# Holding back one transposing load until a weight slice has landed, in a two-layer SiLU block with gradients

## The chip, the cores and the metric

The kernel runs on one core of one Trainium2 chip. The metric is the device time of one execution in microseconds (us), the median over several executions. The profiler's span of an execution is shorter than its time (318.8 against 320.54 for the kernel before); in what follows "span" and "at 18.4 us" are the profile's clock.

## The reference

x is (2048, 640), w1 (640, 1536), w2 (1536, 640), all bf16. The outputs are the result of the block and the gradients for x, w1 and w2.

```python
def _fwd_reference(x, w1, w2):
    h = jnp.einsum("bsd,df->bsf", x, w1)
    h = _silu(h)
    out = jnp.einsum("bsf,fd->bsd", h, w2)
    return out
# reference(): out and the vjp of grad_out for x, w1, w2
```

## The kernel before

The rows of x are worked off in four chunks of 512. For the first chunk the kernel does not wait for one big transposed load: it loads 256 rows plainly and transposes them on TensorE (first half), and gets the other 256 rows (second half) by a transposing DMA. w1 comes in five row slices (k = 0 to 4, the first in two pieces), so that the matmuls of slice k can start as soon as it is there. All loads but two come from the SyncE queue, in the order of the program text:

```python
early += [load_x(nc.sync, 0), load_x(nc.scalar, 1)]
early += [load_w1(0, slice(0, F // 2)), load_w1(0, slice(F // 2, F), nc.scalar)]
early += [load_w1(k) for k in range(1, 3)]
for k in range(3, DT):
    load_w1(k)
nc.sync.dma_start_transpose(out=xT_next[:, :, HC:SC], in_=x2[HC:SC, :])   # second x half
# ...
nc.sync.dma_start(out=w2_nat[:], in_=w2_v[:])                             # w2, 1920 KB
goT_next = load_goT(0)                                                    # transposing
for fc in range(NFC):
    nc.sync.dma_start_transpose(out=w2T[:, :, fc * FC:(fc + 1) * FC], in_=w2[...])
nc.sync.dma_start_transpose(out=w1T[:], in_=w1[:, :])
```

TensorE works through them so (cut):

```python
def h_first(xT, aT, ghT):
    pe_x(xT)                                   # 10 transposes of the first half
    for dt_ in range(DT):                      # first half: slice by slice of w1
        for pair in range(NPAIR):
            h_pair_mm(hs[0][pair], pair, dt_, xT, halves[0])      # 12 matmuls per slice
    # ...
    for pair in range(NPAIR):                  # second half: 60 matmuls, need all of w1 and xT
        for q in range(2):
            for dt_ in range(DT):
                h_pair_mm(hp, pair, dt_, xT, halves[1], (q,))
# then
sd_phase(c, w2_nat, aT, oT_scr)                # "oT" matmuls: the first ones that need w2
```

Of the kernel before, what the change touches and what calls it, by code (L numbers as in the profile page):

```python
# [15 lines left out]
def start_before_entry_wait(nc, names):  # L16




    def move(nc):
        blocks = nc.m.functions[0].blocks
        entry, home = blocks[0].instructions, blocks[1].instructions
        for engine in {i.engine for i in home if i.name in names}:
            mine = [i for i in home if i.engine == engine]
            last = max(k for k, i in enumerate(mine) if i.name in names)
            moved = mine[: last + 1]
            gate = next(
                k
                for k, i in enumerate(entry)  # L30
                if i.engine == engine and isinstance(i, mybir.InstEventSemaphore)
            )
            taken = {i.name for i in moved}
            for k in reversed(range(len(home))):
                if home[k].name in taken:
                    del home[k]
            for i in reversed(moved):
                entry.insert(gate, i)

    nc.at_finalize(move)  # L40


def last_stores_end_on_pool(nc, names):




    def move(nc):
        blocks = nc.m.functions[0].blocks
        stores = [next(i for b in blocks for i in b.instructions if i.name == name) for name in names]  # L50
        lanes = [u.id for i in stores for u in i.sync_info.on_update]
        end = blocks[-1].instructions
        at = next(k for k, i in enumerate(end) if i.engine == mybir.EngineType.SP)
        waits = list(end[at].sync_info.on_wait)
        late = [w for lane in reversed(lanes) for w in waits if w.id == lane]
        assert len(late) == len(names) and not end[at].sync_info.on_update
        waits = [w for w in waits if w.id not in lanes]
        end[at] = copy.replace(end[at], sync_info=mybir.SyncInfo(on_wait=waits, on_update=[]))
        pool = [i for i in end if i.engine == mybir.EngineType.Pool]
        drain, gather, release, reset, clear, drain2, gather2, release2 = pool  # L60
        assert gather2.sync_info.on_wait and not release2.sync_info.on_wait
        assert all(i.sync_info is None or not i.sync_info.on_wait for i in (reset, clear, drain2))
        closing = {i.name for i in (reset, clear, drain2, gather2)}
        to = next(k for k, i in enumerate(end) if i.name == reset.name)
        for k in reversed(range(len(end))):
            if end[k].name in closing:
                del end[k]
        reset = copy.replace(reset, sync_info=mybir.SyncInfo(on_wait=late, on_update=[]))
        for i in (drain2, clear, reset, gather2):
            end.insert(to, i)  # L70

    nc.at_finalize(move)

# [2 lines left out]
def kernel(  # L76
# [11 lines left out]
    nc = tc.nc  # L88
    P = 128
    x2 = x.flatten_outer_dims()  # L90
# [7 lines left out]
    ST, DT, FT = S // P, D // P, F // P  # L98
    SC = 512
# [7 lines left out]
    HC = 2 * P  # L107
# [38 lines left out]
    with ExitStack() as mctx:  # L146
# [9 lines left out]
        early = [nc.vector.memset(warm[:], 1.0)]  # L156
# [13 lines left out]
        def load_xT(c):  # L170
            xT = xpool.tile([P, DT, SC], dt_in, name="xT")
            nc.sync.dma_start_transpose(out=xT[:], in_=x2[c * SC:(c + 1) * SC, :])
            return xT
# [6 lines left out]
        xT_next = xpool.tile([P, DT, SC], dt_in, name="xT")  # L180
# [4 lines left out]
        def load_w1(k, cols=slice(0, F), eng=nc.sync):  # L185
            return eng.dma_start(out=w1_nat[:, k, cols], in_=w1_v[:, k, cols])  # L186
# [1 line left out]
        early += [load_x(nc.sync, 0), load_x(nc.scalar, 1)]  # L188
        early += [load_w1(0, slice(0, F // 2)), load_w1(0, slice(F // 2, F), nc.scalar)]
        early += [load_w1(k) for k in range(1, 3)]  # L190
        for k in range(3, DT):
            load_w1(k)
        nc.sync.dma_start_transpose(out=xT_next[:, :, HC:SC], in_=x2[HC:SC, :])
        start_before_entry_wait(nc, {i.ins.name for i in early})
        nc.scalar.activation(warm_a[:], warm[:, 0:1], ACT.Silu)
        nc.sync.dma_start(out=w2_nat[:], in_=w2_v[:])
# [133 lines left out]
        for c in range(NCH):  # L330
# [4 lines left out]
            if c + 1 < NCH:  # L335
                xT_next = load_xT(c + 1)
# [9 lines left out]
            if c == 0:  # L346
                h_first(xT, aT, ghT)
                nc.sync.dma_start(
                    out=aT_scr[:, c * SC:(c + 1) * SC].rearrange("(ft p) s -> p ft s", p=P), in_=aT[:]
                )  # L350
                sd_phase(c, w2_nat, aT, oT_scr)
                for ft in range(FT):
                    g_group(ft, goT, ghT)
                nc.sync.dma_start(
                    out=ghT_scr[:, c * SC:(c + 1) * SC].rearrange("(ft p) s -> p ft s", p=P), in_=ghT[:]
# [4 lines left out]
            for i in range(FT + LAG):  # L360
# [7 lines left out]
                out=aT_scr[:, c * SC:(c + 1) * SC].rearrange("(ft p) s -> p ft s", p=P), in_=aT[:]  # L368
            )
            nc.sync.dma_start(  # L370
                out=ghT_scr[:, c * SC:(c + 1) * SC].rearrange("(ft p) s -> p ft s", p=P), in_=ghT[:]
# [7 lines left out]
    with ExitStack() as fctx:  # L379
# [17 lines left out]
        k = 0  # L397
# [26 lines left out]
        k = 0  # L424
        for fc in range(NFC):
            gh_blk = gh_blks[fc]
            for dt_ in range(DT):
                if dt_ == DT // 2:
                    store_gw2(fc)
                if fc == NFC - 1 and dt_ == DT - 1:  # L430
                    last_stores = []
                    for k, (lo, hi) in enumerate(((0, FC - P), (FC - P, FC))):
                        gp = ps_h.tile([P, FC], FP32, name="hp")
                        for st in range(ST):
                            nc.tensor.matmul(  # L435
                                gp[:, lo:hi],
                                lhsT=x_nat[:, st, dt_ * P:(dt_ + 1) * P],
                                rhs=gh_blk[:, st, lo:hi],
                                start=(st == 0),
                                stop=(st == ST - 1),  # L440
                            )
                        g1 = s1pool.tile([P, FC], dt_in, name="g1")
                        if k == 0:
                            nc.scalar.activation(g1[:, lo:hi], gp[:, lo:hi], ACT.Copy)
                        else:
                            nc.vector.tensor_copy(out=g1[:, lo:hi], in_=gp[:, lo:hi])  # L446
                        store = nc.sync.dma_start(
                            out=gw1_v[:, dt_, fc * FC + lo:fc * FC + hi], in_=g1[:, lo:hi]
                        )
                        last_stores.append(store.ins.name)  # L450
                    last_stores_end_on_pool(nc, last_stores)
                    continue
# [46 lines left out]
```

## Time and profile before

| | kernel before |
|---|---|
| time, median of 3 runs | 321.04 us (320.81 to 322.33) |
| span of the profiled run | 318.8 us |
| TensorE busy | 313.6 us |
| slice k=2 landed / TensorE waits for it | 7.88 / 0.65 us |
| second x half landed / wanted | 11.12 / 11.76 us |
| w2 landed / first oT matmul | 17.91 / 18.41 us |

The table's landing times come from the trace's records of the semaphore increments (a load counts as landed with the last of its 16), the rest from the views. The prediction below shows the page's lines, the chain of waits and the SyncE queue. One more view is TensorE's timeline of the kernel before, with start, length, line, operation, what, and in brackets the idle time ahead of it and who ended it. L246 are the h matmuls, L315 the oT matmuls.

```profile
5.79 1.48 PE L246 MATMUL hp<-xT,w_nat 128*128 128x256 bf16 x12 [0.22 <-DMA w_nat<-in_w_dram]
7.92 10.65 PE L246 MATMUL hp<-xT,w_nat 128*128 128x256 bf16 x96 [0.65 <-DMA w_nat<-in_w_dram]
18.41 3.83 PE L315 MATMUL hp<-aT,w_nat 128*128 128x512 bf16 x16
```

w2 and w1 carry the same name here (w_nat).

### The profile page before, as it was taken

The numbers are of one execution on the slowest core, as the hardware profiler recorded it, in microseconds if no ns is written. First come the engines' busy times: TensorE is split into PE (matmuls) and PEld (weight loads), VectorE is DVE, ScalarE is ACT, GpSimd is POOL, SyncE is SP. The second block draws the span as 40 slices with busy tenths as digits, with TensorE's granted clock in tenths as the row PEclk, the third lists the DMA queues.
The fourth block names the chain that finished last, engine by engine and source line by source line (L and its number), as shares of the span: only waits on it lengthen the run. The fifth ranks groups of instructions, "written<-read, shape, count | busy, mean of one in ns | idle before, by whom it ended". The sixth has DMA issues, their size and how long they took to land.

```text
span 318.8 us, 3632 instructions
## 1 busy us (share of the span) xinstructions
PE 313.6 (98%) x1516; PEld 150.5 (47%) x1544; DVE 102.8 (32%) x182; ACT 76.8 (24%) x139; POOL 0.7 (0%) x6
## 2 busy tenths in 40 slices
PE   8999999999999999999999999999999999999997
PEld 6854444444444444444444444444444444444444
DVE  1495641477410087710147741000000100001001
ACT  2691000545201354411054520110100001001010
POOL 0000000000000000000000000000000000000000
DMA  8999999999989986492635079909999999997111
GB/s 280 293 181 192 221 249 260 349 252 280 292 214 343 230 155 176 169 310 76 168 110 141 0 256 267 221 20 297 211 245 254 204 251 326 236 313 217 65 35 49
DMA packets 147233, 67.02 MB, mean 210 GB/s; under 512 B 113937, under 2 KB 146705, under 8 KB 147217
## 3 DMA queue, kind: packets, MB, share of 16 engines
q1 hardware_dynamic: 146928, 66.43, 83.3%
q10 hardware_dynamic: 288, 0.36, 0.3%
q8 instruction: 12, 0.20, 0.2%
q14 instruction: 5, 0.03, 0.0%
HBM read 9.18 MB, written 28.97 MB: 120 GB/s over the span
## 4 chain that ended last, share of the span: by engine, by line
PE 96%; DMA 2%; issue 1%; SPq 0%; DVE 0%; DVEq 0%
PE hp L315 32%; PE hp L299 16%; PE hp L404 16%; PE hp L455 15%; PE hp L217 12%; PE hp L246 3%; DMA w_nat<-in_w_dram 2%; PE hp L435 1%; SPq L186 0%; SPq L183 0%; DVE g L446 0%; DVEq L446 0%; SPq L483 0%
## 5 line engine op out<-in xcount | busy, mean ns | idle before, releaser
L299 PE MATMUL hp<-goT,w2T 128*128 128x512 bf16 x239 | 56.8, 379 | 0.1
L315 PE MATMUL hp<-ghT,w1T 128*128 128x512 bf16 x235 | 52.2, 379 | 0.3
L315 PE MATMUL hp<-aT,w_nat 128*128 128x512 bf16 x234 | 52.1, 379 | 0.3
L404 PE MATMUL hp<-a_blk,go_nat 128*128 128x512 bf16 x235 | 51.7, 379 | 0.3
L455 PE MATMUL hp<-gh_blk,x_nat 128*128 128x512 bf16 x219 | 48.2, 379 | 0.3
L217 PE MATMUL hp<-xT,w_nat 128*128 128x512 bf16 x174 | 43.4, 379 | 0.3
L323 ACT ACTIVATE oT<-hp 128x512 bf16<-128x512 f32 x24 | 14.5, 604 | 106.8 <-PE hp L315 106.8
L299 PEld LDWEIGHTS <-w2T 128*128 128x128 bf16 x240 | 23.5, 98 | 28.3
L404 PEld LDWEIGHTS <-go_nat 128*128 128x128 bf16 x240 | 23.5, 98 | 28.3
L315 PEld LDWEIGHTS <-w1T 128*128 128x128 bf16 x240 | 23.4, 98 | 28.4
L315 PEld LDWEIGHTS <-w_nat 128*128 128x128 bf16 x240 | 23.5, 98 | 28.1
L306 DVE SCALAR_TENSOR_TENSOR ghT<-ghT,hp 128x512 bf16<-128x512 bf16 x48 | 32.5, 683 | 7.3 <-PE hp L299 7.3
L455 PEld LDWEIGHTS <-x_nat 128*128 128x128 bf16 x224 | 21.9, 98 | 26.4
L325 DVE CAST oT<-hp 128x512 bf16<-128x512 f32 x16 | 11.1, 691 | 72.2 <-PE hp L315 67.7
L226 ACT ACTIVATE aT<-hp 128x512 bf16<-128x512 f32 x36 | 21.5, 597 | 30.4 <-PE hp L217 30.4
L217 PEld LDWEIGHTS <-w_nat 128*128 128x128 bf16 x180 | 17.6, 98 | 21.2
L233 DVE SCALAR_TENSOR_TENSOR ghT<-aT,v 128x512 bf16<-128x512 bf16 x36 | 24.7, 686 | 0.2
L232 DVE TENSOR_SCALAR v<-t 128x512 bf16<-128x512 f32 x36 | 15.4, 427 | 26.7 <-ACT t L230 26.7
L230 ACT ACTIVATE t<-hp 128x512 f32<-128x512 f32 x36 | 21.3, 591 | 0.0
L466 DVE CAST g<-hp 128x512 bf16<-128x512 f32 x7 | 4.8, 692 | 47.0 <-PE hp L455 27.0
L414 DVE CAST g2T<-hp 128x512 bf16<-128x512 f32 x7 | 4.8, 692 | 46.1 <-PE hp L404 46.1
L412 ACT ACTIVATE g2T<-hp 128x512 bf16<-128x512 f32 x8 | 4.8, 597 | 47.0 <-PE hp L404 47.0
(28 smaller groups left out, 76.4 us busy)
## 6 DMA issues: line engine op xcount, KB each, us to landing
aT_scr<-aT SPq DMA_DIRECT2D x4, 1536.0 KB, 6.3
ghT_scr<-ghT SPq DMA_DIRECT2D x4, 1536.0 KB, 8.2
out_dram<-o_sb SPq DMA_DIRECT2D x8, 640.0 KB, 3.3
oT_scr<-oT SPq DMA_DIRECT2D x4, 640.0 KB, 3.6
go_nat<-in_grad_out_dram SPq DMA_DIRECT2D x4, 640.0 KB, 8.1
gxT_scr<-oT SPq DMA_DIRECT2D x4, 640.0 KB, 4.8
w_nat<-in_w_dram SPq DMA_DIRECT2D x1, 1920.0 KB, 11.0
x_nat<-in_x_dram SPq DMA_DIRECT2D x3, 640.0 KB, 7.4
```

Source lines behind the costliest of these rows:

```text
L217: nc.tensor.matmul(hp[:], lhsT=w1_nat[:, dt_, ft * P:(ft + 1) * P], rhs=xT[:, dt_, :], start=(dt_ == 0), stop=(dt_ == DT - 1),)
L226: nc.scalar.activation(aT[:, ft, :], hp[:], ACT.Silu)
L230: nc.scalar.activation(t[:], hp[:], ACT.Tanh, scale=0.5)
L232: nc.vector.tensor_scalar(out=v[:], in0=t[:], scalar1=-0.5, scalar2=0.5, op0=ALU.mult, op1=ALU.add)
L233: nc.vector.scalar_tensor_tensor(out=ghT[:, ft, :], in0=aT[:, ft, :], scalar=1.0, in1=v[:], op0=ALU.subtract, op1=ALU.mult)
L299: nc.tensor.matmul(gp[:], lhsT=w2T[:, dt_, ft * P:(ft + 1) * P], rhs=goT[:, dt_, :], start=(dt_ == 0), stop=(dt_ == DT - 1),)
L306: nc.vector.scalar_tensor_tensor(out=ghT[:, ft, :], in0=ghT[:, ft, :], scalar=1.0, in1=gp[:], op0=ALU.add, op1=ALU.mult)
L315: nc.tensor.matmul(op_[:], lhsT=w_all[:, ft, dt_ * P:(dt_ + 1) * P], rhs=rhs_all[:, ft, :], start=(ft == 0), stop=(ft == FT - 1),)
L323: nc.scalar.activation(oT[:, dt_, :], op_[:], ACT.Copy)
L325: nc.vector.tensor_copy(out=oT[:, dt_, :], in_=op_[:])
L404: nc.tensor.matmul(gp[:], lhsT=go_nat[:, st, dt_ * P:(dt_ + 1) * P], rhs=a_blk[:, st, :], start=(st == 0), stop=(st == ST - 1),)
L455: nc.tensor.matmul(gp[:], lhsT=x_nat[:, st, dt_ * P:(dt_ + 1) * P], rhs=gh_blk[:, st, :], start=(st == 0), stop=(st == ST - 1),)
```

## The change

The intent: the second x half isn't wanted before 11.8 us, the w1 slices are wanted at once. If the descriptors of the early-issued transposing load (its orders for the single pieces) stand in the way of the w1 slices, hold that load back until the third slice (k=2) has landed. With the change, the lines stand 25 lower (L246 is L271, L315 is L340, L196 is L221), the transposing load itself 24 (L193 is L217).

```diff
+def issue_after_landing(nc, name, load_name):
+    def move(nc):
+        insts = [i for b in nc.m.functions[0].blocks for i in b.instructions]
+        load = next(i for i in insts if i.name == load_name)
+        (lane,) = {u.id for u in load.sync_info.on_update}
+        first = min(
+            (w for i in insts if i.sync_info is not None for w in i.sync_info.on_wait if w.id == lane),
+            key=lambda w: w.wait_value,
+        )
+        # ... adds `first` to the waits of the instruction `name`
+    nc.at_finalize(move)
...
-        for k in range(3, DT):
-            load_w1(k)
-        nc.sync.dma_start_transpose(out=xT_next[:, :, HC:SC], in_=x2[HC:SC, :])
+        late = [load_w1(k) for k in range(3, DT)]
+        x_late = nc.sync.dma_start_transpose(out=xT_next[:, :, HC:SC], in_=x2[HC:SC, :])
+        issue_after_landing(nc, x_late.ins.name, early[-1].ins.name)
```

More of the change, by code (lines that the diff above doesn't have):

```diff
@@ L70, in move @@
             end.insert(to, i)
+    nc.at_finalize(move)
[8 more added lines that the diff above has]
+        )
+        for block in nc.m.functions[0].blocks:
+            for k, i in enumerate(block.instructions):
+                if i.name == name:
+                    have = i.sync_info
+                    waits = [] if have is None else list(have.on_wait)
+                    updates = [] if have is None else list(have.on_update)
+                    assert all(w.id != lane for w in waits)
+                    block.instructions[k] = copy.replace(
+                        i, sync_info=mybir.SyncInfo(on_wait=waits + [first], on_update=updates)
+                    )
     nc.at_finalize(move)
```

## The prediction

> **What bounds the kernel now.** I read the page first, then the chain of waits in order of time, then the waits by engine, then the first 32 us of the timeline by engine, and last the landing times of the single DMAs.
>
> The page says where a change can count at all:
>
> ```profile
> span 318.8 us, 3632 instructions
> PE 313.6 (98%) x1516; PEld 150.5 (47%) x1544; DVE 102.8 (32%) x182; ACT 76.8 (24%) x139; POOL 0.7 (0%) x6
> PE 96%; DMA 2%; issue 1%; SPq 0%; DVE 0%; DVEq 0%
> ```
>
> TensorE is busy 313.6 of 318.8 us, so only 5.2 us are idle in the whole kernel, start and tail included. No change to a load can win more than that, and one that wins 2% (6.4 us) is out of reach. The 2% of DMA on the chain that ended last is the part to look at. In order of time the chain reads:
>
> ```profile
> 1.47 6.41 DMA w_nat<-in_w_dram
> 7.88 0.05 issue
> 7.92 10.65 PE hp L246 x96
> ...
> 18.84 10.74 PE hp L315 x49
> ...
> 31.53 8.85 PE hp L299 x41
> ```
>
> The columns are start, length, what. The DMA is the third w1 row slice (k=2), issued at 1.47 and landed at 7.88. From 7.92 on TensorE runs through with gaps of hundredths of a us. So anything that moves 7.92, or opens a gap after it, reaches the end one for one. The waits of the first 40 us give the size of what there is to win:
>
> ```profile
> PE hp L246 <- DMA w_nat<-in_w_dram: 0.9, 2, 0.7
> ```
>
> TensorE waits 0.22 us for slice k=1 (before 5.79) and 0.65 us for slice k=2 (before 7.92), together 0.87 us. The queue of SyncE is the other half of the story; in its timeline the columns are start, length of the issue, what:
>
> ```profile
> 0.54 2.31 SPq L186 DMA_DIRECT2D w_nat<-in_w_dram  x5
> 3.09 3.79 SPq L193 DMA_TRANSPOSE xT<-in_x_dram  x1
> 6.94 0.58 SPq L196 DMA_DIRECT2D w_nat<-in_w_dram  x1
> 7.56 10.61 SPq L177 DMA_TRANSPOSE goT<-in_grad_out_dram  x1
> 18.21 10.18 SPq L199 DMA_TRANSPOSE w2T<-in_w_dram  x3
> 28.43 9.14 SPq L200 DMA_TRANSPOSE w1T<-in_w_dram  x1
> ```
>
> The transposing load of the second x half is issued at 3.09, right behind slices k=3 and k=4, its issue occupies the queue for 3.79 us, and it lands 8.0 us after its start, at 11.1. All of it is in-order: the w2 load starts only at 6.94.
>
> **What the Trainium skill says.** "Perfetto Trace Analysis", section "DMA Instruction — HWDGE (DVE, Sync)", says that the profiled length of such an issue is descriptor generation, that the data movement [...]is not in it. The trace agrees: L193 is 3.79 us long and lands 4.2 us after its end. "DMA: Bandwidth & Descriptors", section "Queues, rings and completion order", says that one copy is split over the rings of up to 16 engines and that each ring consumes its descriptors in order. The trace agrees in that the 256-byte packets of the transpose begin in number only at 7.5 us, when most engines have used up their w1 packets. The same page, section "Why a DMA increments its semaphore by 16 and not by 1", says that the engines finish independently and only the full count means landed. This is what makes 7.88: of the 16 increments of slice k=2 thirteen are in by 6.70, the others come at 7.18, 7.39 and 7.88. In the packet records one 3072-byte packet, started at 4.68, took 2.05 us where its neighbours take 0.12; two others, at 3.42 and 3.45, took 1.0 us. One late engine sets the landing.
>
> **The change part by part.** It removes, adds and moves no work: the same DMAs with the same bytes. It adds one wait to the issue of L193, for the full count of slice k=2. Call the landing of that slice L2 (7.88 before).
>
> 1. SyncE stands still from about 2.9 us to L2. The transpose starts at L2 + 0.05 instead of 3.09.
>
> 2. Its issue should be shorter than 3.79. A transposing load of twice the rows takes 3.24 to 3.49 us on this queue (L199), so half takes about 1.7 us (estimate); the 3.79 held some waiting for room behind the late engine.
>
> 3. Its landing: in steady state a transposing load lands 2.3 to 3.0 us after its issue ends (L199's three: 21.70 to 24.17, 24.98 to 28.01, 28.39 to 31.40; one of L136: 124.72 to 126.97). So the half lands about 1.7 + 2.3 to 3.0 = 4.0 to 4.7 us after L2.
>
> 4. When it is needed: the first half takes dt 2, 3 and 4 after L2, 3 x 12 matmuls at 10.65 / 96 = 0.111 us, so 4.0 us. Before, the second half began at about 7.92 + 4.0 = 11.9, and the load had landed at 11.1, hidden with 0.8 us in hand. After, it arrives 0.0 to 0.7 us after the moment when TensorE wants it. So the hidden load becomes the next bound, at about L2 + 4.3, and the net change at this place is (L2 - 7.88) + about 0.3.
>
> 5. The w2 load is issued behind it. Its packets began at 10.05 before (when those of the transpose ended) and it landed 7.9 us later, at 17.91, with TensorE asking for it at 18.3 to 18.4: only 0.4 us in hand. After, its packets begin at about L2 + 0.05 + 1.7 + 1.4 = L2 + 3.1 and it lands at about L2 + 11.0; TensorE asks at L2 + 4.3 + 6.5 = L2 + 10.8. So this wait adds 0.2 at the most, near a tie.
>
> 6. Later loads slip by up to 1 us. w2T's first piece landed at 24.2 and is wanted at 31.2; w1T landed at 40.5 and is wanted at 44.1; the next xT landed at 43.9 and is wanted at 57. All have 3.6 us or more in hand: no cost.
>
> 7. What can be won is L2 itself. If the descriptors of the transpose held up the w1 packets (the 1 to 2 us packets come 0.3 to 1.6 us after its issue began), their removal lets the last engine keep up with the thirteen good ones: L2 about 6.7. Then TensorE no longer waits at all for k=2: dt 2 starts right after dt 1, at about 7.1 to 7.3. That is a gain of 0.6 to 0.9 us, less 0.0 to 0.3 for step 4 (with L2 = 6.7 the load lands at 10.7 to 11.4, wanted at 11.2).
>
> Sum: if L2 falls to 6.7, -0.5 to -0.8 us; if it falls to 7.3, about -0.3; if it stays at 7.88, +0.3 to +0.6.
>
> **The rivals.** First, the long packets have nothing to do with the transpose. For it: later transposes are issued beside plain loads (the grad_out one beside w2 from 7.56 on) and the longest plain packet there is 0.47 us; and plain loads at 77 to 81 us show packets of 0.3 to 0.8 us with no transpose being issued just then. Ring order also means that a transpose cannot overtake w1. Against it: the three worst plain packets of the whole kernel fall just after this issue. Then L2 is 7.88 or scatters by itself, and the change costs about 0.5 us: 321.5. Second, the wait takes the place of the one removed: TensorE saves 0.65 us at k=2 and gives it back before the second half; then the time stays at 321.0. The margin of 0.8 us in step 4 against a delay of the issue of 3 us or more speaks for at least a part of this. Third, the w2 load becomes the bound: if its packets start later than I reckon (a second late engine, or the instruction fetch of 1.07 us that fell into it at 13.94), TensorE stands for up to 1.5 us before the second stage, 322.0 or so. Its 0.4 us in hand speaks for it.
>
> **Range and chances.** I give the first reading of step 7 a little over one half, because somebody wrote exactly this wait for exactly this slice, and because the worst packets sit where they do; the rivals share the rest. 0.55 x -0.6 + 0.25 x +0.0 + 0.20 x +0.6 is about -0.2 us, so 321.04 - 0.2 = 320.8. The three times before spread over 1.5 us by themselves (320.81 to 322.33), more than the change can move, so the range is 320.0 to 322.0. Faster or slower by over 2% would be 6.4 us, more than all idle time and more than any wait above: 1% each, as allowance for a surprise.
>
> **What would show it right or wrong.** In the changed kernel: the wait of L193 for w_nat should be about 4 us, ending at the landing of k=2; its issue should be 1.6 to 2.0 us long (right for step 2) and not 3.8. The wait of TensorE for k=2 should shrink from 0.65 to near 0 if step 7 is right; if it is still 0.6 us, the first rival is. A new wait of L246 for the transposing load of xT, near 11.5 us, shows step 4; its absence shows that I overrated the landing. The start of the first L315 matmul, 18.41 before, sums all of it up: 17.6 to 17.9 if I am right, 18.9 or later if the rivals are. A new wait of L315 for w_nat shows the third rival. The prediction would be wrong as a whole if the first L315 start moved by over 1 us, or if the span moved without it.

## The result

| | before | after |
|---|---|---|
| time, median of 6 runs each | 320.75 us (320.25 to 322.33) | 320.95 us (320.75 to 321.33) |
| ratio | | 1.0002 (95%: 0.998 to 1.0024) |
| profiled span | 318.8 us | 319.4 us |

A ratio here is the mean time of one kernel's fast runs over that of the other's of the same rounds, so not quite the ratio of the medians. The result is "the same", inside the predicted range. Later rounds with the unchanged pair (below) make it 1.0015 and 1.0024, so that the changed kernel is, if anything, some tenths of a us slower; only the last of the three intervals (1.0005 to 1.0043) leaves out 1. Of all runs, 7 of 45 of the kernel before and 2 of 18 of the changed one lie 0.7 us or more above the median of their group, which widens every interval; what happens in those runs stays open.

The page of the kernel after:

```profile
span 319.4 us, 3661 instructions
PE 315.9 (99%) x1544; PEld 150.7 (47%) x1544; DVE 102.8 (32%) x182; ACT 76.8 (24%) x139; POOL 0.7 (0%) x6
```

The instruction counts of the two pages differ by 28 matmul records that are missing from the trace before (1516 of 1544) and by one waiting instruction, which the change adds on SyncE's queue; the work is the same. The chain of waits after, in order of time, and the SyncE queue's timeline:

```profile
1.47 6.00 DMA w_nat<-in_w_dram
...
7.54 1.42 SPq L217
...
9.01 9.96 DMA w_nat<-in_w_dram
...
19.01 13.12 PE hp L340 x60
```

```profile
0.53 2.31 SPq L211 DMA_DIRECT2D w_nat<-in_w_dram  x5
7.54 1.42 SPq L217 DMA_TRANSPOSE xT<-in_x_dram  x1
9.01 0.57 SPq L221 DMA_DIRECT2D w_nat<-in_w_dram  x1
9.63 9.62 SPq L202 DMA_TRANSPOSE goT<-in_grad_out_dram  x1
```

The chain has changed its route. Before, it ran from slice k=2 straight into TensorE and stayed there. Now it runs slice k=2, the issue of the transpose, the w2 load, and only then TensorE: the new wait has put SyncE and w2 on the path. w2 is issued at 9.01 instead of 6.94. TensorE's timeline after shows the price:

```profile
3.90 14.61 PE L271 MATMUL hp<-xT,w_nat 128*128 128x256 bf16 x120 [0.18 <-DMA w_nat<-in_w_dram]
19.01 3.20 PE L340 MATMUL hp<-aT,w_nat 128*128 128x512 bf16 x14 [0.50 <-DMA w_nat<-in_w_dram]
```

The wait for slice k=2 is gone from the list, and yet the h matmuls end hardly earlier (the last one's weights are loaded at 18.13, before 18.20): in this run it was the second piece of slice 0 (5.28 instead of 4.12) and slice 1 (6.50 instead of 5.74) that came late. TensorE came to k=2 late by itself. And the first oT matmul now waits for w2, which landed at 18.96. It starts at 19.01 against 18.41; the span is 0.60 longer, exactly that.

That equality is the best instrument. In all 13 profiles, those of the experiments too, the span less the start of the first oT matmul is 300.33 to 300.36 us. Whatever happens in the first 18 us reaches the end through this one number, and nothing behind it moves. So each profile can be read to 0.03 us, although the times scatter by a us. The h matmuls' last weights ("h end" in the table below) are loaded 0.21 to 0.22 us before the first oT matmul where nothing is waited for; what goes beyond that is the wait for w2: 0.67 us in this run, none in the kernel before.

### The profile page after: what moved, and what is told of

Read it like the earlier page. It is cut to its first block, busy times and chain, and to the rows that moved or that the text cites. A ratio compares the mean times of both kernels' runs of the same rounds, so it can differ in the third digit from the quotient of the medians.

```text
span 319.4 us, 3661 instructions
## 1 busy us (share of the span) xinstructions
PE 315.9 (99%) x1544; PEld 150.7 (47%) x1544; DVE 102.8 (32%) x182; ACT 76.8 (24%) x139; POOL 0.7 (0%) x6
## 4 chain that ended last, share of the span: by engine, by line
PE 93%; DMA 5%; SPq 1%; issue 0%; DVE 0%; DVEq 0%
PE hp L340 32%; PE hp L429 16%; PE hp L324 16%; PE hp L480 15%; PE hp L242 12%; DMA w_nat<-in_w_dram 5%; PE hp L460 1%; SPq L217 0%; SPq L211 0%; SPq L208 0%; DVE g L471 0%; DVEq L471 0%; SPq L508 0%
## 5 line engine op out<-in xcount | busy, mean ns | idle before, releaser
L340 PE MATMUL hp<-aT,w_nat 128*128 128x512 bf16 x240 | 52.5, 379 | 0.5 <-DMA w_nat<-in_w_dram 0.5
L340 PE MATMUL hp<-ghT,w1T 128*128 128x512 bf16 x240 | 52.5, 379 | 0.0
L340 PEld LDWEIGHTS <-w_nat 128*128 128x128 bf16 x240 | 23.4, 98 | 28.9 <-DMA w_nat<-in_w_dram 0.8
L340 PEld LDWEIGHTS <-w1T 128*128 128x128 bf16 x240 | 23.5, 98 | 28.3
```

The costliest lines, as they stand in the source:

```text
L340: nc.tensor.matmul(op_[:], lhsT=w_all[:, ft, dt_ * P:(dt_ + 1) * P], rhs=rhs_all[:, ft, :], start=(ft == 0), stop=(ft == FT - 1),)
```

## The experiments

Four theories were put to the test. A: the early issue of the transpose slows the w1 slices (the intent of the change). B: the slices are delayed by chance, by a few long packets, whatever is issued. (A packet is one piece of a load in the trace, here a row of 1280 to 3072 bytes.) C: what the change costs is the later w2 load. E: the goT transpose, now issued just as w2's packets begin, draws them out. Eleven runs were made, each with a profile and timed in five rounds; those of one group share a chip and the runs of the kernel before.

The table gathers all 13 profiles, from the trace's records; in us. "Long" counts plain packets (1280 to 3072 bytes) of over 0.5 us that started between 2.9 and 6.5 us, while w1 moves. "xT" is the second x half; "xT wanted" is the first weight load of the second half, "h end" the last h weight load.

| kernel | k=2 landed | long | xT landed / wanted | w2 issued / landed | h end | first oT | span |
|---|---|---|---|---|---|---|---|
| before | 7.88 | 6 | 11.12 / 11.76 | 6.94 / 17.91 | 18.20 | 18.41 | 318.76 |
| before_again | 7.38 | 9 | 10.62 / 11.26 | 6.26 / 17.41 | 17.70 | 17.92 | 318.27 |
| before_w2_halves | 7.57 | 7 | 10.78 / 11.72 | 6.57 / 13.90, 17.70 | 18.16 | 18.38 | 318.71 |
| before_w2_late | 7.44 | 7 | 10.64 / 11.32 | 8.51 / 17.65 | 17.76 | 17.98 | 318.32 |
| before_w2_late2 | 7.49 | 5 | 10.71 / 11.37 | 8.51 / 17.53 | 17.81 | 18.03 | 318.38 |
| before_w2_later | 7.68 | 3 | 10.88 / 11.56 | 9.66 / 18.32 | 18.00 | 18.36 | 318.71 |
| after | 7.46 | 7 | 10.99 / 11.69 | 9.01 / 18.96 | 18.13 | 19.01 | 319.36 |
| after_again | 7.79 | 10 | 11.44 / 11.66 | 9.32 / 18.81 | 18.11 | 18.85 | 319.21 |
| after_third | 8.24 | 8 | 12.14 / 12.47 | 9.91 / 19.28 | 18.91 | 19.33 | 319.68 |
| after_w2_halves | 7.27 | 13 | 10.93 / 11.25 | 8.82 / 16.30, 18.98 | 17.69 | 17.91 | 318.24 |
| after_goT_late | 7.51 | 8 | 11.21 / 11.51 | 9.06 / 18.63 | 17.95 | 18.67 | 319.03 |
| wait_k1 | 7.73 | 8 | 10.95 / 12.00 | 8.35 / 18.90 | 18.44 | 18.94 | 319.30 |
| wait_k4 | 7.46 | 12 | 14.47 / 14.51 | 10.89 / 20.40 | 20.86 | 21.07 | 321.41 |

### The same two kernels once more

No edit. The kernel before against itself:

> The kernel before, unchanged, against itself: a null test and a second profile of it. Theory A (the transpose's early issue slows the w1 slices): slice k=2 lands again near 7.9 us and TensorE waits 0.6 us or more for it. Theory B (a few plain packets of 0.5 to 2 us come with the first big w1 packets whatever is issued, and which slice they delay is chance): k=2 lands somewhere between 6.7 and 7.9, again with 4 to 9 plain packets over 0.5 us between 2.9 and 6.5 us. Both: w2 lands near 17.9 and isn't waited for. Time 1.000 of before, within 0.2%.

The changed kernel:

> The changed kernel, unchanged: a second profile of it and a tighter interval. Theory A: k=2 lands by 7.0 to 7.5 and fewer long packets than in the kernel before between 2.9 and 6.5 us (3 or less). Theory B: k=2 lands between 6.7 and 7.9 and again 4 to 9 long packets there. Theory C (what the change costs is the later w2 load): w2 lands L2 + 11 or so (18.0 to 19.0) and TensorE waits 0.2 to 0.8 us for it at the first oT matmul. Time 1.000 to 1.002 of before.

Measured: the kernel before against itself 320.50 us, ratio 0.9991 (0.9975 to 1.0008); so this is how exact a ratio of 1 comes out. The changed kernel 320.98 us, 1.0015 (0.9995 to 1.0035). TensorE's timelines, the kernel before first:

```profile
5.84 12.24 PE L246 MATMUL hp<-xT,w_nat 128*128 128x256 bf16 x108 [0.39 <-DMA w_nat<-in_w_dram]
17.92 4.26 PE L315 MATMUL hp<-aT,w_nat 128*128 128x512 bf16 x19
```

```profile
7.83 10.65 PE L271 MATMUL hp<-xT,w_nat 128*128 128x256 bf16 x96 [0.36 <-DMA w_nat<-in_w_dram]
18.85 3.41 PE L340 MATMUL hp<-aT,w_nat 128*128 128x512 bf16 x15 [0.37 <-DMA w_nat<-in_w_dram]
```

Read the first line of each. In these two runs the roles are swapped: it is the changed kernel that waits for slice k=2 until 7.8, and the kernel before that starts at 7.4 (inside its merged line). The 7.88 on which my prediction built was one draw. Theory A expected 3 long packets or less with the transpose held back; there were 10. That the landing scatters without regard to the transpose is shown; that the long packets cause the scatter, as theory B has it, is not: over the table the most long packets (13) go with the earliest landing of k=2 (7.27), and the fewest (3) with 7.68. The second line of the changed kernel has the wait for w2 again.

### w2 in two loads

```diff
-        nc.sync.dma_start(out=w2_nat[:], in_=w2_v[:])
+        nc.sync.dma_start(out=w2_nat[:, 0:FT // 2, :], in_=w2_v[:, 0:FT // 2, :])
+        nc.sync.dma_start(out=w2_nat[:, FT // 2:FT, :], in_=w2_v[:, FT // 2:FT, :])
```

On the kernel before:

> The kernel before with the w2 load cut into two DMAs of six row blocks each, so that the first oT matmuls need only the first half. In the kernel before w2 was not waited for, so theory C expects no gain: 0.999 to 1.001. The first oT matmul starts where the h matmuls end (about 18.4) and w2 is not waited for.

On the changed kernel:

> The changed kernel with the same cut of the w2 load. Theory C: the wait of 0.5 to 0.8 us before the first oT matmul vanishes (first oT matmul at 18.0 to 18.5 instead of 19.0) and the time falls by 0.3 to 0.7 us against the changed kernel of these rounds. If it is theory B alone (nothing but chance), it equals the changed kernel within 0.1%, because the wait for w2 was a stroke of this one profile.

Measured: before_w2_halves 320.65 us, 1.0004 (0.9977 to 1.0031); after_w2_halves 320.28 us, 0.9997 (0.9969 to 1.0025), against 320.98 of the changed kernel in the same rounds. The medians are 0.70 apart, the means 0.57 (320.64 and 321.21), as theory C expected; no interval was computed for this pair. Five runs of six of the one (320.03 to 320.38) lie below all of the other (320.79 and up), the sixth (322.84) lies above them all, so the times alone do not prove it. SyncE's timeline of the changed kernel with halves, then TensorE's:

```profile
8.82 0.57 SPq L221 DMA_DIRECT2D w_nat<-in_w_dram  x1
9.44 0.54 SPq L222 DMA_DIRECT2D w_nat<-in_w_dram  x1
```

```profile
6.11 11.96 PE L272 MATMUL hp<-xT,w_nat 128*128 128x256 bf16 x108 [0.42 <-DMA w_nat<-in_w_dram]
17.91 4.26 PE L341 MATMUL hp<-aT,w_nat 128*128 128x512 bf16 x19
```

The second half of w2 still lands at 18.98, as late as in the changed kernel, but the oT matmuls begin at 17.91, right after the h matmuls, with what is there at 16.30. So the wait for w2 is real. Not all of the gain is the cut's: the first oT matmul starts 0.94 us earlier than in after_again, of which 0.42 is that the h matmuls ended earlier (17.69 against 18.11, the slices' chance) and only 0.52 the wait that went. Read in this way, the wait cost about 0.7, 0.5 and 0.2 us in the three profiles of the changed kernel, about what it loses. On the kernel before, where there was no such wait, the same edit gains nothing that the rounds could tell.

### Only w2 later

The transpose goes out early as before; only the w2 load, and with it all that stands behind it in the queue, waits: for slice k=3, or for k=4.

```diff
-        nc.sync.dma_start(out=w2_nat[:], in_=w2_v[:])
+        w2_load = nc.sync.dma_start(out=w2_nat[:], in_=w2_v[:])
+        issue_after_landing(nc, w2_load.ins.name, late[0].ins.name)   # before_w2_late; late[1] in before_w2_later
```

> One part alone: the transpose is issued early as in the kernel before; only the w2 load (and all loads behind it) waits, for slice k=3, so that it is issued at 8.3 to 8.9 us as in the changed kernel (9.0 to 9.3). Theory C (the later w2 load is the whole cost): w2 lands near 18.8, the first oT matmul starts near 18.9 instead of 17.9 to 18.4, time as the changed kernel, 1.0010 to 1.0020 of before. Rival (the later transpose itself costs): no loss, 0.999 to 1.0005. Theory E (the goT transpose, issued just as the first w2 packets move, draws them out): 3 to 10 plain packets over 0.5 us after 10 us, where the kernel before had 0 and 0.

Measured: 320.39 us, 0.9986 (0.9964 to 1.0008). This went against theory C as I had put it: w2 was issued 1.6 us later than in the kernel before and landed at 17.65, no later than there. Two more runs followed, in one group with the changed kernel, to see whether this was luck and whether a still later issue costs:

> The kernel with w2 alone waiting for slice k=3 once more, for a second profile: w2 issued at 8.4 to 8.7. If the first profile was typical, w2 lands at 17.5 to 18.0 and there is no loss (0.998 to 1.0005); if it was luck, w2 lands near 18.5 and the time is between the two kernels.

> Transpose early as in the kernel before; the w2 load waits for the last slice (k=4), so it is issued at about 9.4 us, a little later than in the changed kernel (9.0 and 9.3), where w2_late had 8.5. Theory C' (the w2 load's issue time sets its landing, with some slack up to about 8.5): w2 lands at 18.7 to 19.1, its packets ramp up over 1 us or more, the first oT matmul waits 0.5 to 0.9 us, time as the changed kernel or a little over it, 1.001 to 1.002. Theory F (the late transpose is needed for the loss): w2 lands by 18.1 and the time is that of the kernel before.

> The changed kernel in the same rounds, for the comparison: w2 issued at 9.0 to 9.4, landed at 18.6 to 19.0, first oT matmul waits 0.5 to 0.8 us; time 1.001 to 1.002 of before.

Measured: before_w2_late2 320.73 us, 0.9995 (0.998 to 1.0011); before_w2_later 320.99 us, 1.0009 (0.9991 to 1.0027); after_third 321.48 us, 1.0024 (1.0005 to 1.0043). SyncE's timeline of before_w2_late2:

```profile
2.99 3.43 SPq L217 DMA_TRANSPOSE xT<-in_x_dram  x1
8.51 0.40 SPq L220 DMA_DIRECT2D w_nat<-in_w_dram  x1
```

The same of before_w2_later, and below it a line of its waits (who waited for whom: us in total, times, longest):

```profile
3.00 3.25 SPq L217 DMA_TRANSPOSE xT<-in_x_dram  x1
9.66 0.40 SPq L220 DMA_DIRECT2D w_nat<-in_w_dram  x1
```

```profile
PEld L340 <- DMA w_nat<-in_w_dram: 0.3, 1, 0.3
```

before_w2_late2 has no such line: its waits end with the h matmuls.

So the issue time of w2 has slack. The packets of w2 stand behind those of the transpose, which ended at 10.1 to 10.6 us when it was issued early; issued by 8.5 us, w2 began at 9.8 to 10.3 and landed at 17.4 to 17.9 in all five profiles. Issued at 9.66, it began at 10.7, landed at 18.32 and was waited for by 0.3 us. The changed kernel issues it at 9.0 to 9.9, later than the 8.5 that is shown to be free, and in addition its transpose ends later (packets to 10.5 to 11.6). It landed there at 18.8 to 19.3, later than the issue alone gives: in the first profile of the changed kernel it was issued earlier than in before_w2_later (9.01 against 9.66) and began earlier (10.27 against 10.72), and yet landed later (18.96 against 18.32). So the later issue is not the whole cause of the later landing. The timed ratios go the same way (0.9986 and 0.9995, then 1.0009, then 1.0024), but the intervals of the last three overlap; the ordering rests on the profiles.

### goT held back

```diff
-        goT_next = load_goT(0)
+        goT_next = xpool.tile([P, DT, SC], dt_in, name="goT")
+        goT_load = nc.sync.dma_start_transpose(out=goT_next[:], in_=go2[0:SC, :])
+        issue_after_landing(nc, goT_load.ins.name, w2_load.ins.name, 1)   # waits for w2's landing
```

> The changed kernel, with the goT transpose issued only once w2 has landed. Theory E: no plain packet over 0.5 us after 10 us; w2's packets need 7.1 us from first to last as in the kernel before (7.6 to 8.2 in the changed one), it lands near 17.9 to 18.3 and the wait before the first oT matmul falls to 0.3 us or less; time 0.3 to 0.7 us below the changed kernel. If the long packets come from something else, w2 lands at 18.7 to 19.0 again and the time equals the changed kernel's. goT then lands near 23.5 and the last w2T piece near 34: both still in time (31.2, 39.8), unless w1T, near 43, comes late for 44.1.

Measured: 320.87 us, 1.0002 (0.9977 to 1.0028). SyncE's timeline, then TensorE's:

```profile
18.69 2.85 SPq L225 DMA_TRANSPOSE goT<-in_grad_out_dram  x1
```

```profile
18.67 3.63 PE L344 MATMUL hp<-aT,w_nat 128*128 128x512 bf16 x16 [0.34 <-DMA w_nat<-in_w_dram]
```

With no transpose being issued between 9.0 and 18.69, w2 was nearly as late as ever (18.63 against 18.81 to 19.28), and 8 of its packets were over 0.5 us. Theory E is out by this profile; the time, whose interval holds both answers, does not decide. The increments of w2's semaphore came one by one here: 15 of the 16 were in by 18.02, the last came at 18.63. (goT, issued 9 us later than in the changed kernel, cost nothing, as its margins said.)

### Another slice to wait for

```diff
-        issue_after_landing(nc, x_late.ins.name, early[-1].ins.name)
+        issue_after_landing(nc, x_late.ins.name, early[-2].ins.name)   # wait_k1; late[1] in wait_k4
```

> The changed kernel with the wait for the second w1 slice (k=1) in place of the third: the transpose is issued near 5.8 to 6.5 us, w2 near 7.4 to 8. Theory C: w2 lands at 17.8 to 18.4 and is waited for by 0.3 us or less; the time lies between the two kernels, 0.9995 to 1.001 of before. The transpose lands by 10.5 to 11 and isn't waited for.

> The changed kernel with the wait for the last slice (k=4), near 9.4 to 9.9. Now the transpose lands at 12.9 to 13.4, wanted at 11.7 to 11.9: a new wait of the h matmuls for xT of 1.0 to 1.6 us. w2 lands at 20.2 to 20.9; the first oT matmul starts there. Theory C: +1.8 to +2.5 us over the kernel before, 1.006 to 1.008. If only the transpose's own wait counted: +1.0 to +1.6. If neither: no change.

Measured: wait_k1 321.11 us (320.24 to 322.63), 1.0009 (0.9981 to 1.0036): inconclusive by its time, and its profile has w2 at 18.90 where I expected 17.8 to 18.4: a miss. w2 was issued at 8.35 there and began at 10.18, both earlier than some of the kernels in which it landed by 17.9 (issued at 8.51 in before_w2_late, begun at 10.33 in the kernel before), so neither its issue nor its first packet explains this landing. wait_k4 323.32 us (321.88 to 325.12; the two longest, 325.12 and 324.65, at clock 0.995), 1.0085 (1.005 to 1.012), a little over the 1.006 to 1.008 expected. SyncE's timeline of wait_k4, then TensorE's:

```profile
9.43 1.42 SPq L217 DMA_TRANSPOSE xT<-in_x_dram  x1
```

```profile
14.51 6.72 PE L271 MATMUL hp<-xT,w_nat 128*128 128x256 bf16 x60 [2.55 <-DMA xT<-in_x_dram]
21.07 1.24 PE L340 MATMUL hp<-aT,w_nat 128*128 128x512 bf16 x5
```

Here at last the transpose itself is the bound, by 2.55 us, more than the 1.0 to 1.6 expected: it landed 5.0 us after its issue, where 3.5 to 3.8 were usual in the changed kernel, and the trace has a 16 KB instruction fetch of 1.12 us in the middle of its packets. w2, landed at 20.40, was not waited for; so the mechanism that I had put down for most of the loss (w2) was not the one that acted.

## Why the prediction was right or wrong

**The time and the range** were right: 320.8 predicted, 320.95 measured, and "the same" for the reason given (only 5.2 us of idle time in the kernel, and a change that moves waits of tenths of a us). That the two numbers are only 0.15 us apart is luck: 320.8 was 321.04 less a gain of 0.2, there was no gain, and the kernel before came out at 320.75 over six runs.

**The direction** was not. I leaned to a gain of 0.2 us; against the kernel before of the same rounds, the mean of the changed kernel's runs was +0.07, +0.34 and +0.74 us in the three groups, on average +0.4 us.

**Step 7 failed** (what can be won is the landing of slice k=2, because the transpose's descriptors hold up the w1 packets). It put the landing at 6.7 once the transpose was out of the way. In the six profiles with the transpose early, k=2 landed at 7.38 to 7.88, mean 7.57; in the seven with it held back at 7.27 to 8.24, mean 7.64. Long packets numbered 3 to 9 before and 7 to 13 after. The first rival of the prediction was right: the long packets do not come from the transpose. I had read the position of three packets in one trace as a cause. The sign that was to show step 7 right, TensorE's wait for k=2 near 0, did appear in the first profile, but by luck: slice 1 came so late (6.50) that TensorE asked for k=2 only 0.30 us after it had landed (7.76 against 7.46). The sign that sums up, the start of the first oT matmul, was clear: 19.01, where "18.9 or later" stood for the rivals. (A smaller misreading: at 7.5 us it was not most engines that had used up their w1 packets; 14 w1 packets and 2 of the transpose were in flight, and 3 and 15 only at 8.5 us. That the transpose moves in as w1 runs out is so. And its sum was loose: from 7.92 to 7.1 to 7.3 is 0.6 to 0.8 us, and less 0.0 to 0.3 that leaves 0.3 to 0.8, not 0.5 to 0.8.)

**Step 2** (shorter issue) was right: 1.41 to 1.72 us, estimated at 1.7. What the longer issue before was waiting for, no run shows.

**Step 4 failed in size.** The held-back load landed 3.5 to 3.9 us after k=2 (in the five profiles of that wait), not 4.0 to 4.7, and was wanted 3.9 to 4.2 us after it. The margin was 0.2 to 0.7 us, and the second rival, a wait for xT in the place of the one removed, did not come, except in wait_k4, where it was forced. My estimate took the tail after an issue (2.3 to 3.0 us) from loads of twice the length; here it was 2.0 to 2.3.

**Step 5 was right in the landing and wrong in the wait.** w2 landed 11.50, 11.02 and 11.04 us after k=2 in the three profiles of the changed kernel, against 11.0 predicted; TensorE asked for it 10.78, 10.43 and 10.78 us after k=2, against 10.8. So the weight loads of the first oT matmul waited 0.8, 0.6 and 0.3 us, not 0.2 at most (0.1 us more than the matmuls lost, since a weight load usually runs that much ahead of its matmul: 18.31 and 18.41 in the kernel before). The excess has two sources: in the first profile w2 took 8.70 us from its first packet to its landing, where the prediction reckoned with 7.9; in the second TensorE came earlier, because xT did not hold it up. (In the first and the third it would have come earlier too, but for the late slice 1, which made it start k=2 0.30 us after the landing.) The start of w2's packets before was misread besides: the first one is at 10.33, not 10.05, so that they took 7.58 us and not 7.9. The third rival, w2 as the new bound, is what happened, if with 0.3 to 0.8 us and not 1.5. after_w2_halves shows it: the same kernel without this wait is back at the time of the kernel before.

**Step 6** was right: nothing behind the first oT matmul moved, to 0.03 us.

What stays open: why w2 lands later in the changed kernel than its issue alone explains. Its long packets are one trail. From issue to first packet there were 2.9 to 3.6 us in the three kernels with an early w2 and in wait_k4, and their w2 packets of over 0.3 us add up to 0.0 to 0.7 us; in the other nine the lead was 1.1 to 1.8 us and the sum 3.2 to 11.3 us. That is a correlation; the goT run takes away one explanation, and it doesn't settle the landing. Another division goes with the landing better: from its first packet to its landing w2 took 7.6 to 7.8 us in all six kernels that issue the transpose early (with 10.8 us of long packets in before_w2_later), and 7.9 to 8.8 in the six that hold it back for k=1 or k=2 (with 4.6 us of long packets in wait_k1, where it took 8.7); in wait_k4 it took 6.6. So the late landing goes with the held-back transpose, beyond the issue time of w2. What the link is, no run shows; the one late increment in after_goT_late makes a single slow engine a candidate.

## What to carry to other kernels

A queue that issues in order passes a wait on to everything behind it (here w2 and goT, each 2.07 us later in the first profile): before holding back a load, look up the slack of the loads behind it, not only of the load itself. A single late packet in one trace is a draw, not a cause; profile the unchanged kernel twice before building on its position. Where one load only just makes its moment, cutting it so that its first part is enough takes it off the path (here it brought the changed kernel back to about the level of the kernel before).

## What the Trainium skill lacked or had wrong

- "DMA: Bandwidth & Descriptors", section "DMA Transpose (X-bar)": nothing on whether the transpose's packets wait for an engine that is late. The trace looks like it, though it doesn't name the engine of a packet. In the kernel before, sixteen 256-byte packets of the transpose that started between 7.9 and 8.8 us took 0.9 to 1.8 us each, against 0.02 elsewhere, and all ended at 9.6 to 9.7, shortly after the last w1 packet (9.47); the sixteen increments of slice k=4 arrived together at 9.75 to 9.83. With the transpose held back, the increments of k=4 were spread over 7.66 to 9.45, and no packet of the transpose took over 0.5 us in the five profiles of that wait.
- The same page, section "Latency and other measured facts", gives an HBM access latency of up to 2 us at high load. Single plain packets of 0.5 to 2.05 us, where 0.12 is usual, appeared in every one of the 13 profiles (3 to 13 of them between 2.9 and 6.5 us). Whether they are that latency no run shows, nor how far they set the landing of a slice. That the slowest of the engines decides is as its section "Why a DMA increments its semaphore by 16 and not by 1" says, and the trace agrees: of the 16 increments of slice k=2 in the kernel before, thirteen were in by 6.70 us, the last at 7.88.
- No page gives what an instruction fetch costs a load beside it: the 16 KB fetches of the first 20 us took 0.93 to 1.5 us each. In wait_k4 one (11.71 to 12.83) fell into the 256-row transpose, which took 2.95 us from its first packet to its last against 1.6 to 1.9 in the changed kernel. It is one case.
- "Perfetto Trace Analysis", section "DMA Instruction — HWDGE (DVE, Sync)", says that the profiled length is that of the issue, a wait for the descriptor generator included, and leaves out the movement of the data. The trace agrees (L193 ends at 6.89 us and its load lands at 11.12). The page gives no size for what can come on top when much is queued ahead: the same transpose took 1.4 to 1.7 us to issue once k=1 or a later slice had landed and 3.06 to 3.79 us behind four w1 slices.
